# Block means by a second accumulated product instead of a broadcast transfer, in the first four units of a sparse attention followed by two gated layers

## The chip, the cores and the metric

One core of one Trainium2 chip. The metric is device time in microseconds (us) of one execution; the time of a kernel is the median over its runs. The profile is of one further execution, whose own time and span stand in the table below. The engines are PE (TensorE), DVE (VectorE), ACT (ScalarE), POOL (GpSimd) and SP, which in this kernel only issues transfers.

## The reference

Attention over 2 batches, 8 heads, 768 positions of 64 numbers, then two dense gated layers on 1536 tokens. Each query sees its neighbours closer than 16 positions and one summary for every block of 32 positions: the largest key of the block and the mean of its values.

```python
k_sum = k.reshape(B, H, nb, block, D).max(axis=3)
v_sum = v.reshape(B, H, nb, block, D).mean(axis=3)
...
scores_all = np.concatenate([scores_l_m, scores_s], axis=-1)
...
v_all = np.concatenate([v, v_sum], axis=2)
return np.matmul(a, v_all).astype(np.float32)
...
x = _moe_ref(x=x, **moe_kwargs)
return _moe2_ref(x=x, **moe2_kwargs)
```

## The kernel before

The attention is cut into 24 units: 2 batches, 3 groups of four query blocks (64 queries each), 4 pairs of heads. Units 0 to 3 are the first group, 4 to 7 the second, and so on; batch 1 begins with unit 12. One unit goes through these steps, each a function:

- `w_copy` (POOL, tile `kx`): the window of 96 keys of each query block, and ahead of it 32 columns for the block maxima (`ks`, made by DVE in `prep_k`).
- `b_pe` (PE, L556 and L558, tile `ps_s`): a product that adds the mask, then four score products of the unit's queries `q` with `kx`. `b_max` (DVE, `nm`), `b_exp` (ACT, `e`), `n_inv` (DVE) and `n_mul` (POOL) make the weights.
- `c_pe` (PE, L591, `ps_p`) transposes them, `c_copy` (ACT for the first ten units, `pt`) copies them out.
- `d_pe` (PE, L606, `ps_x`): eight products per unit of `pt` with `vwin`. `d_hi` (ACT, `xH`) and `d_lo` (DVE, `xL`) split the result into two parts for the dense layers.

`vwin` has eight slots of 128 rows, four for one group and four for the next: rows 32 to 127 hold the window's values, loaded by `load_v` (L495), and rows 0 to 31 the block means, which `put_v` (L500) copies into all four slots of a group by a transfer from the tile `vsum` (named `vs` in the trace). The means come from `sum_load` (transfers, `vt`), `sum_v` (DVE sums, `vm`), and `sum_lay` (four PE products `ps_v`, then ACT at L530). For batch 0, `put_v(0, 0)` and `put_v(0, 1)` are issued by ACT, the others by SP.

Weights of the dense layers come by `fetch` (L165, 1 MB pieces named `raw`, one in the tile `xH`) and are decoded into two parts each by DVE and ACT (`decode`, L102 to L112). Their products are at L349; those of the first layer on the first 512 tokens can begin when units 0 to 7 are done.

The order on PE, DVE, ACT and POOL is set by a scheduler when the program is built, so an edit at one place can move instructions elsewhere; each engine then runs its list in order. SP's list stands in the order in which the code is written. The query loads of units 0 to 3 are issued by ACT, all other loads by SP. The transfers share eight completion semaphores in turn: a transfer that takes one waits until its last user has landed. Queries have five buffers, so the load of unit u waits for the scores of unit u - 5. The first `load_v` of batch 0's third group overwrites the slots of the first group, and waits in SP's list for the last `ps_x` of unit 3; behind it stand that group's `put_v`, the queries of unit 13, and the weight piece `raw_1_1` of `moe_w_out`.

Of the kernel before, what the change touches and what calls it, by code (L numbers as in the profile page):

```python
# [8 lines left out]
F32 = mybir.dt.float32  # L9
# [3 lines left out]
AF = mybir.ActivationFunctionType  # L13
# [3 lines left out]
P = 128  # L17
# [11 lines left out]
def attention_moe_moe2_kernel(ctx: ExitStack, tc: tile.TileContext, ins: dict, out: bass.AP):  # L29
    nc = tc.nc  # L30
# [4 lines left out]
    B, HP, _, S = vt.shape  # L35
    H, D = 2 * HP, 64
    BLK = 32
# [4 lines left out]
    W0 = 32  # L42
    M0 = W0 + HALO
    G = 4
# [7 lines left out]
    scale = 1.0 / float(D) ** 0.5  # L52
# [98 lines left out]
    for layer, g, i in wanted:  # L151
        w = mats[layer][i]
        last = i == len(mats[layer]) - 1
        x = w.bitcast(U32)
        pieces.append((f"{layer}_{g}_{i}", rows_of(x, g) if last else cols_of(x, g, 2)))

    def fetch():

        if pieces:
            name, src = pieces.pop(0)  # L160
            n, m = src.shape[1], src.shape[2]

            home, tag = (xp, "xH") if name == "1_0_1" else (wraw, "raw")
            raw = home.tile([P, n * m], U32, tag=tag, name=f"{tag}{name}")
            nc.sync.dma_start(out=raw.rearrange("p (a n) -> p a n", a=n), in_=src)  # L165
            raws.append((raw, (P, n, m // 2)))
# [279 lines left out]
    def pull(n):  # L446
        for _ in range(n):
            if next(coming, True):
                break
# [5 lines left out]
    with tc.manual_schedule(engines={mybir.EngineType.SP}), ExitStack() as es:  # L455
# [6 lines left out]
        vp = es.enter_context(tc.tile_pool(name="a_v", bufs=1))  # L462
        ps_a = es.enter_context(tc.tile_pool(name="ps_a", bufs=1, space=PSUM))

        vwin = one.tile([P, 2 * G, H * D], F32, name="vwin")
# [4 lines left out]
        qbd, vsum, kraw, kmax, kx = {}, {}, {}, {}, {}  # L470
        SH = S + 2 * HALO

        def load_k(b, hp):

            t = kp.tile([P, SH], F32, tag="k", name=f"k{b}_{hp}")
            nc.sync.dma_start(out=t, in_=k[b, hp])
            kraw[b, hp] = t

        def load_q(u, eng):

            b, g, hp = units[u]
            t = qp.tile([P, G, P], F32, tag="q", name=f"q{u}")
            eng.dma_start(out=t.rearrange("p i c -> p (i c)"), in_=q[b, g, hp])
            qbd[u] = t

        def vw(b, i):
            return vwin[:, (b * NG + i // G) % 2 * G + i % G, :]

        def load_v(b, g):
            c = (b * NG + g) % 2 * G  # L490
            first_row = v[b, g * G * QB:g * G * QB + P - W0, :]
            src = bass.AP(
                first_row.tensor, first_row.offset, [first_row.ap[0], [QB * H * D, G], [1, H * D]]
            )
            nc.sync.dma_start(out=vwin[W0:P, c:c + G, :], in_=src)  # L495

        def put_v(b, g, eng=nc.sync):
            c = (b * NG + g) % 2 * G
            src = vsum[b].unsqueeze(1).to_broadcast([W0, G, H * D])
            eng.dma_start(out=vwin[0:W0, c:c + G, :], in_=src)  # L500

        vtl, vpart = {}, {}

        def sum_load(b, hp):
            if (b, hp) == (0, 2):
                early = xp.tile([P, 2, KC * TB // 2], F32, tag="xL", name="vt_early")
                vtl["early"] = [early[:, i, 0:S] for i in range(2)]
            if b == 0 and hp > 1:
                t = vtl["early"][hp - 2]
            else:  # L510
                t = vp.tile([P, S], F32, tag="vt", bufs=2, name=f"vt{b}_{hp}")
            nc.sync.dma_start(out=t, in_=vt[b, hp])
            vtl[b, hp] = t

        def sum_v(b, hp):
            if hp == 0:
                vpart[b] = vp.tile([P, HP, W0], F32, tag="vm", name=f"vm{b}")
                nc.vector.memset(vpart[b], 0.0)
            nc.vector.tensor_reduce(
                out=vpart[b][:, hp, 0:NB], in_=vtl.pop((b, hp)).rearrange("p (n t) -> p n t", t=BLK),  # L520
                axis=AX.X, op=ALU.add,
            )

        def sum_lay(b):
            r = vpart.pop(b)
            vsum[b] = vp.tile([W0, H * D], F32, tag="vs", name=f"vs{b}")
            ps = ps_a.tile([W0, H * D], F32, tag="x", name="ps_v", bufs=2)
            for hp in range(HP):
                nc.tensor.matmul(ps[:, hp * P:(hp + 1) * P], lhsT=r[:, hp], rhs=ident, start=True, stop=True)
            nc.scalar.activation(vsum[b], ps, AF.Copy, scale=1.0 / BLK)  # L530

        def prep_k(b, hp):
            ks = kp.tile([P, W0], F32, tag="ks", name=f"ks{b}_{hp}")
            nc.vector.memset(ks, 0.0)
            own = kraw[b, hp][:, HALO:HALO + S].rearrange("p (n t) -> p n t", t=BLK)
            nc.vector.tensor_reduce(out=ks[:, 0:NB], in_=own, axis=AX.X, op=ALU.max)
            kmax[b, hp] = ks
# [61 lines left out]
        def d_pe(u):  # L599
            b, g, hp = units[u]  # L600
            t = live.pop(("pt", u))
            ps = ps_a.tile([P, G, QB], F32, tag="x", name="ps_x", bufs=2)
            for j in range(G):
                for e in range(2):
                    h = 2 * hp + e
                    nc.tensor.matmul(  # L606
                        ps[64 * e:64 * e + 64, j, :],
                        lhsT=vw(b, g * G + j)[:, h * D:(h + 1) * D],
                        rhs=t[:, j, 64 * e:64 * e + 64],
                        start=True, stop=True,  # L610
                    )
            live["x", u] = ps.rearrange("p j c -> p (j c)")

        def x_slice(x, u):
# [11 lines left out]
        def d_lo(u):  # L626
# [6 lines left out]
        ORDER = [  # L633
            (w_copy, -1), (b_pe, 0), (b_max, 0), (n_inv, LN), (n_mul, LN),
            (c_pe, LC), (c_copy, LC), (d_pe, LD), (d_hi, LD), (b_exp, 0), (d_lo, LD),
        ]


        warm = one.tile([P, TB], BF16, name="warm")
        nc.vector.memset(warm, 0.0)  # L640
        for _ in range(4):
            ps = ps_h.tile([P, TB], F32, tag="h", name="ps_w")
            nc.tensor.matmul(ps, lhsT=warm[:, 0:P], rhs=warm, start=True, stop=True)
# [52 lines left out]
        for t in range(-1, NU + LD):  # L696
            now[0] = t

            u = t + 2
            if u < NU and units[u][1] == 0:  # L700
                prep_k(units[u][0], units[u][2])
            for part, lag in ORDER:
                if 0 <= t - lag < NU:
                    part(t - lag)
            if 0 <= t < NU - 5:
                load_q(t + 5, nc.sync)
            if t == -1:
                sum_v(0, 0)
                sum_v(0, 1)
            if t == 0:  # L710
                sum_v(0, 2)
                sum_v(0, 3)
                sum_lay(0)
                put_v(0, 0, nc.scalar)
                load_v(0, 1)
                put_v(0, 1, nc.scalar)
                fetch()
            if t in (5, 8):
                fetch()
            if t in (7, 8, 9, 10):  # L720
                sum_load(1, t - 7)
            if t in (8, 9, 10, 11):
                sum_v(1, t - 8)
            if t == 11:
                sum_lay(1)

            if t % HP == HP - 1 and HP < t < NU - HP:
                c = t // HP + 1
                load_v(c // NG, c % NG)
                put_v(c // NG, c % NG)  # L730
            if 8 <= t < 8 + HP:
                load_k(1, t - 8)
            if t >= 1:
                pull(1 if t < 6 or t > 9 else 2)
            for _ in range(2 if t >= 8 else 1):
                next(fill, None)
# [3 lines left out]
    with tc.manual_schedule(engines={mybir.EngineType.SP}):  # L740
# [11 lines left out]
        for step in steps[EARLY:]:  # L752
            layer, g, blk = step
# [91 lines left out]
```

## Time and profile before

| | before |
|---|---|
| median of 3 runs | 639.03 us (637.85 to 639.6) |
| the profiled execution, its time | 637.64 us |
| its span | 635.8 us |
| PE busy | 611.7 us (96%) |
| DVE busy | 431.8 us (68%) |
| ACT busy | 283.2 us (45%) |
| POOL busy | 194.3 us (31%) |

PE is busy nearly all the time after the first 70 us; the profiled execution's time lies 1.8 us above its span. Times within the trace count from the span's start.

### The profile page before, as it was taken

The numbers are of one execution on the slowest core, as the hardware profiler recorded it, in microseconds if no ns is written. First come the engines' busy times: TensorE is split into PE (matmuls) and PEld (weight loads), VectorE is DVE, ScalarE is ACT, GpSimd is POOL, SyncE is SP. The second block draws the span as 40 slices with busy tenths as digits, with TensorE's granted clock in tenths as the row PEclk, the third lists the DMA queues.
The fourth block names the chain that finished last, engine by engine and source line by source line (L and its number), as shares of the span: only waits on it lengthen the run. The fifth ranks groups of instructions, "written<-read, shape, count | busy, mean of one in ns | idle before, by whom it ended". The sixth has DMA issues, their size and how long they took to land.

```text
span 635.8 us, 8219 instructions
## 1 busy us (share of the span) xinstructions
PE 611.7 (96%) x3098; PEld 499.7 (79%) x3098; DVE 431.8 (68%) x628; ACT 283.2 (45%) x560; POOL 194.3 (31%) x164
## 2 busy tenths in 40 slices
PE   7488999999999999999999999999999999999997
PEld 4376777778888888888888887888887888888886
DVE  6788665378987575566359996169499479496524
ACT  2587676736543333323144745444344244343310
POOL 6885676313313231322222121030031030130210
PEclk9899899999999999999999999999999999999999
DMA  9989653014542212100002304012122112200004
GB/s 307 330 269 333 227 134 67 2 66 149 183 132 67 66 67 66 67 1 1 0 1 66 109 25 132 1 66 66 67 67 74 59 67 66 68 0 1 1 34 165
DMA packets 25304, 58.33 MB, mean 92 GB/s; under 512 B 1585, under 2 KB 1841, under 8 KB 25265
## 3 DMA queue, kind: packets, MB, share of 16 engines
q1 hardware_dynamic: 24400, 56.24, 27.3%
q10 hardware_dynamic: 864, 1.57, 0.7%
q8 instruction: 24, 0.39, 0.3%
q14 instruction: 16, 0.12, 0.1%
HBM read 53.08 MB, written 3.15 MB: 88 GB/s over the span
## 4 chain that ended last, share of the span: by engine, by line
PE 82%; DVE 7%; ACT 3%; DMA 3%; POOL 2%; issue 2%; SPq 0%; ACTq 0%; DVEq 0%; POOLq 0%
PE ps_o L349 34%; PE ps_h L349 19%; PE ps_v L124 8%; PE ps_y L124 7%; PE ps_x L124 5%; PE ps_h L124 4%; PE ps_s L558 3%; DMA raw<-in_moe_w_out 2%; POOL kx L547 1%; PE ps_x L606 1%; DVE wf L205 1%; DVE ws L214 1%; DMA vt<-in_vt 1%; PE ps_p L591 1%; DVE sg L364 1%
## 5 line engine op out<-in xcount | busy, mean ns | idle before, releaser
L366 POOL TENSOR_TENSOR gl<-sg,gh 128x512 fp32r<-128x512 f32 x84 | 119.5, 1424 | 404.3 <-ACT gh L365 381.0
L429 DVE TENSOR_TENSOR acc<-ps_o,acc 128x512 f32<-128x512 f32 x143 | 97.2, 686 | 57.2 <-PE ps_o L349 57.1
L365 ACT CAST gh<-sg 128x512 fp32r<-128x512 f32 x84 | 51.9, 620 | 91.7 <-DVE sg L364 81.2
L349 PE MATMUL ps_h<-xL,w_0H 128*128 128x512 f32 x192 | 75.1, 391 | 1.5 <-DVE xL L627 1.5
L349 PE MATMUL ps_h<-xH,w_0L 128*128 128x512 f32 x192 | 75.1, 394 | 0.3 <-DVE acc L429 0.3
L349 PE MATMUL ps_o<-gl,w_1H 128*128 128x512 f32 x192 | 75.3, 392 | 0.1
L349 PE MATMUL ps_o<-gh,w_1L 128*128 128x512 f32 x192 | 74.8, 398 | 0.2 <-DVE sg L364 0.2
L349 PE MATMUL ps_o<-gh,w_1H 128*128 128x512 f32 x192 | 74.8, 390 | 0.0
L349 PE MATMUL ps_h<-xH,w_0H 128*128 128x512 f32 x192 | 74.8, 389 | 0.0
L364 DVE TENSOR_TENSOR sg<-ps_h,sg 128x512 f32<-128x512 f32 x48 | 33.0, 687 | 47.0 <-ACT sg L373 46.9
L349 PE MATMUL ps_o<-w_2H,gl 128*128 128x512 f32 (+1 forms) x146 | 56.2, 389 | 1.0 <-ACT acc L425 0.6
L349 PE MATMUL ps_o<-w_2L,gh 128*128 128x512 f32 (+1 forms) x146 | 56.4, 386 | 0.0
L349 PE MATMUL ps_o<-w_2H,gh 128*128 128x512 f32 (+1 forms) x146 | 56.4, 386 | 0.0
L373 ACT ACTIVATE sg<-ps_h 128x512 f32<-128x512 f32 x48 | 28.4, 595 | 60.7 <-PE ps_h L349 60.6
L107 DVE SCALAR_TENSOR_TENSOR da<-da,db 128x1024 uint32<-128x1024 uint32 x34 | 43.8, 1287 | 13.8 <-ACT da L103 13.5
L103 ACT ACTIVATE da<-da 128x1024 f32<-128x1024 f32 x34 | 36.1, 1060 | 32.6 <-DVE da L102 29.8
L349 PEld LDWEIGHTS ps_h<-xL,w_0H 128*128 128x128 f32 x192 | 36.1, 188 | 9.1 <-DVE xL L627 1.9
L349 PEld LDWEIGHTS ps_h<-xH,w_0L 128*128 128x128 f32 x192 | 36.0, 188 | 8.0 <-DVE acc L429 0.8
L349 PEld LDWEIGHTS ps_o<-gh,w_1L 128*128 128x128 f32 x192 | 36.1, 189 | 7.8 <-DVE sg L364 0.5
L349 PEld LDWEIGHTS ps_o<-gl,w_1H 128*128 128x128 f32 x192 | 36.1, 188 | 7.6 <-POOL gl L366 0.4
L349 PEld LDWEIGHTS ps_o<-gh,w_1H 128*128 128x128 f32 x192 | 36.1, 188 | 7.3
L349 PEld LDWEIGHTS ps_h<-xH,w_0H 128*128 128x128 f32 x192 | 36.0, 188 | 7.3
(157 smaller groups left out, 1236.5 us busy)
## 6 DMA issues: line engine op xcount, KB each, us to landing
raw<-in_moe_w_out SPq DMA_DIRECT2D x13, 1024.0 KB, 4.8
raw<-in_moe_w_in SPq DMA_DIRECT2D x8, 1024.0 KB, 7.3
raw<-in_moe_w_gate SPq DMA_DIRECT2D x6, 1024.0 KB, 5.1
raw<-in_moe_w_val SPq DMA_DIRECT2D x6, 1024.0 KB, 5.2
q<-in_q SPq DMA_DIRECT2D x20, 256.0 KB, 7.8
vwin<-in_v SPq DMA_DIRECT2D x6, 768.0 KB, 7.8
k<-in_k SPq DMA_DIRECT2D x8, 400.0 KB, 7.3
out<-acc SPq DMA_DIRECT2D x11, 256.0 KB, 2.0
```

The source lines that it names most:

```text
L103: nc.scalar.activation(af, af, AF.Prelu, scale=REBIAS, alpha=-2.0 ** 32)
L107: nc.vector.scalar_tensor_tensor(out=a, in0=a, scalar=3, in1=b, op0=ALU.logical_shift_left, op1=ALU.bitwise_or)
L124: nc.tensor.matmul(ps, lhsT=a[x][:, kk, :], rhs=b[y][:, kk, :], start=start and i == 0, stop=i == n - 1, skip_group_check=True,)
L205: nc.vector.tensor_tensor(out=w.rearrange(flat), in0=hi.rearrange(flat), in1=lo.rearrange(flat), op=ALU.add)
L214: nc.vector.tensor_tensor(out=s[:, n], in0=a, in1=b, op=op)
L349: nc.tensor.matmul(ps, lhsT=a, rhs=b, start=i == 0, stop=i == n - 1)
L364: nc.vector.tensor_tensor(out=sg, in0=val, in1=sg, op=ALU.mult)
L365: nc.scalar.copy(gh, sg)
L366: nc.gpsimd.tensor_tensor(out=gl, in0=sg, in1=gh, op=ALU.subtract)
L373: nc.scalar.activation(sg, ps, AF.Sigmoid, scale=1.702 if layer == 1 else 1.0)
L429: nc.vector.tensor_tensor(out=a[:, m, :], in0=ps, in1=a[:, m, :], op=ALU.add)
L558: nc.tensor.matmul(ps[:, j, :], lhsT=t[:, j, :], rhs=kt[:, j, :], start=False, stop=j == G - 1)
```

## The change

The tile `vsum` gets 128 rows and a buffer for each batch. ACT fills, at the start, rows 0 to 31 of the first four slots of `vwin` and the whole of batch 0's `vsum` with zeros, from the zero tile `warm`; later `sum_lay` writes the means into rows 0 to 31 of `vsum`, and the rest stays zero. Units 0 to 3 then take two products into the same accumulator: `pt` with `vwin`, whose mean rows are zero, and `pt` with `vsum`, whose window rows are zero. The transfer `put_v(0, 0)` is no longer issued. All other units work as before.

```diff
         def put_v(b, g, eng=nc.sync):
             c = (b * NG + g) % 2 * G
-            src = vsum[b].unsqueeze(1).to_broadcast([W0, G, H * D])
+            src = vsum[b][0:W0].unsqueeze(1).to_broadcast([W0, G, H * D])
             eng.dma_start(out=vwin[0:W0, c:c + G, :], in_=src)
...
+        for b in range(B):
+            vsum[b] = vp.tile([P, H * D], F32, tag="vs", bufs=B, name=f"vs{b}")
...
         def sum_lay(b):
             r = vpart.pop(b)
-            vsum[b] = vp.tile([W0, H * D], F32, tag="vs", name=f"vs{b}")
...
-            nc.scalar.activation(vsum[b], ps, AF.Copy, scale=1.0 / BLK)
+            nc.scalar.activation(vsum[b][0:W0], ps, AF.Copy, scale=1.0 / BLK)
...
                     h = 2 * hp + e
-                    nc.tensor.matmul(
-                        ps[64 * e:64 * e + 64, j, :],
-                        lhsT=vw(b, g * G + j)[:, h * D:(h + 1) * D],
-                        rhs=t[:, j, 64 * e:64 * e + 64],
-                        start=True, stop=True,
-                    )
+                    parts = [(vw(b, g * G + j), t)]
+                    if (b, g) == (0, 0):
+                        parts.append((vsum[b], t))
+                    for n, (x, y) in enumerate(parts):
+                        nc.tensor.matmul(
+                            ps[64 * e:64 * e + 64, j, :],
+                            lhsT=x[:, h * D:(h + 1) * D],
+                            rhs=y[:, j, 64 * e:64 * e + 64],
+                            start=n == 0, stop=n == len(parts) - 1,
+                        )
...
         nc.vector.memset(warm, 0.0)
+        nc.scalar.copy(vwin[0:W0, 0:G, :], warm[0:W0].unsqueeze(1).to_broadcast([W0, G, H * D]))
+        nc.scalar.copy(vsum[0], warm)
...
                 sum_lay(0)
-                put_v(0, 0, nc.scalar)
                 load_v(0, 1)
                 put_v(0, 1, nc.scalar)
```

The scheduler moves the products of units 0 to 3. In the order of before they all stand behind the scores of units 6 and 7. These are rows of PE's list of before, from the mask product ahead of unit 6 on (`kx6`, `q6` belong to unit 6; `ps_x_302`, `_348`, `_391`, `_435` are units 0, 1, 2, 3):

```order
L556 MATMUL ps_s_464<-mask_110,pick_111 128x512
L558 MATMUL ps_s_415<-kx6_368,q6_246 128x128 x4
L556 LDWEIGHTS pick_111
L556 MATMUL ps_s_513<-mask_110,pick_111 128x512
L558 MATMUL ps_s_464<-kx7_412,q7_276 128x128 x4
L606 MATMUL ps_x_302<-pt_300,vwin_109 64x64 x8
L606 MATMUL ps_x_348<-pt_346,vwin_109 64x64 x8
L558 MATMUL ps_s_513<-kx8_461,q8_321 128x128 x4
L591 MATMUL ps_p_428<-ident_67,e_315 128x128 x4
L606 MATMUL ps_x_391<-pt_389,vwin_109 64x64 x8
L606 MATMUL ps_x_435<-pt_433,vwin_109 64x64 x8
```

Now the first product of unit 0 (`ps_x_304`, line 611 of the changed file) stands ahead of the scores of units 3 and 4, and its partner with `vs0` behind the transposes of unit 1:

```order
L611 MATMUL ps_x_304<-pt_302,vwin_109 64x64
L530 MATMUL ps_v_213<-ident_67,vm0_185 32x128
L559 MATMUL ps_s_338<-kx4_281,q4_150 128x128 x4
L559 MATMUL ps_s_284<-kx3_256,q3_142 128x128 x4
L530 MATMUL ps_v_213<-ident_67,vm0_185 32x128
L592 MATMUL ps_p_351<-ident_67,e_243 128x128 x4
L611 MATMUL ps_x_304<-pt_302,vs0_112 64x64
```

From there the pairs of units 0 and 1 follow one another, then the scores of unit 5, then the pairs of unit 2. Further on in the changed list, the last pair of unit 2 (`ps_x_409`) comes just ahead of the scores of units 6 and 7, and unit 3 (`ps_x_461`) just behind:

```order
L611 MATMUL ps_x_409<-pt_407,vs0_112 64x64
L559 MATMUL ps_s_441<-kx6_386,q6_248 128x128 x4
L559 MATMUL ps_s_498<-kx7_438,q7_278 128x128 x4
L557 LDWEIGHTS pick_111
L557 MATMUL ps_s_547<-mask_110,pick_111 128x512
L611 MATMUL ps_x_461<-pt_459,vwin_109 64x64
L611 MATMUL ps_x_461<-pt_459,vs0_112 64x64
```

So three of the four units moved ahead of unit 6's scores, and the fourth ahead of unit 8's. The second place is the head of ACT's list. Before, it issues four query loads and then loads its function table:

```order
L483 DMA q0_122<-in_q 128x512
L483 DMA q1_126<-in_q 128x512
L483 DMA q2_132<-in_q 128x512
L483 DMA q3_138<-in_q 128x512
L571 ACT_TABLE_LOAD
```

In the changed list the table load and the two zero copies stand between the second and the third query load:

```order
L483 DMA q0_126<-in_q 128x512
L483 DMA q1_130<-in_q 128x512
L646 ACT_TABLE_LOAD
L646 CAST vwin_109<-warm_114 32x2048
L647 CAST vs0_112<-warm_114 128x512
L483 DMA q2_136<-in_q 128x512
L483 DMA q3_142<-in_q 128x512
```

The table load is the same one, moved ahead. SP's list keeps its order over the stretch that the prediction speaks of.

## Rows read from the trace of the kernel before

**Rows 1.** Chain of work that ended last, 30 to 60 us: start, length, what.
```profile
34.24 1.32 PE ps_x L606 x32
...
37.11 0.59 ACT pt L596
...
40.37 10.12 DMA raw<-in_moe_w_out
...
50.51 0.69 DVE db L105
```

**Rows 2.** Stretches: busy time (and instructions) by engine, then clock, DMA share, GB/s.
```profile
20.00:30.00 10.00, 3.40 (x21) 2.03 (x20) 8.16 (x13) 7.38 (x28) 9.94 (x9) 0.89 1.05 301
30.00:36.00 6.00, 5.94 (x53) 5.53 (x54) 4.74 (x9) 2.97 (x5) 4.58 (x5) 0.61 1.04 369
36.00:38.00 2.00, 1.94 (x34) 1.63 (x35) 1.66 (x6) 1.16 (x5) 1.93 (x2) 1.00 0.80 284
38.00:40.00 2.00, 1.86 (x27) 1.55 (x23) 1.55 (x5) 2.00 (x9) 1.36 (x2) 1.00 0.25 40
40.00:42.00 2.00, 1.08 (x8) 0.65 (x7) 2.00 (x4) 2.00 (x11) 1.58 (x2) 1.00 0.74 202
42.00:50.00 8.00, 7.07 (x82) 6.17 (x83) 5.18 (x12) 7.73 (x35) 4.60 (x4) 1.00 1.05 320
50.00:60.00 10.00, 8.53 (x74) 6.38 (x72) 9.49 (x17) 5.90 (x19) 6.32 (x6) 1.00 1.05 387
...
32.00:34.00 2.00, 2.00 (x10) 1.85 (x8) 1.86 (x2) 0.31 (x1) 2.00 (x3) 0.50 1.06 389
```

**Rows 3.** Timeline of PE, 20 to 36 us: start, length, what, idle before and releaser.
```profile
22.25 1.16 PE L558 MATMUL ps_s<-kx,q 128*128 128x128 f32 x8
...
30.06 2.05 PE L558 MATMUL ps_s<-kx,q 128*128 128x128 f32 x8 [3.50 <-POOL e L585]
...
32.32 1.91 PE L558 MATMUL ps_s<-kx,q 128*128 128x128 f32 x8
34.17 1.39 PE L606 MATMUL ps_x<-pt,vwin 128*64 128x64 f32 x32
```

**Rows 4.** Timeline of POOL, 26 to 30 us.
```profile
26.43 0.53 POOL L547 TENSOR_SCALAR kx<-ks 128x128 f32<-128x128 f32 x1
26.93 3.02 POOL L585 TENSOR_TENSOR e<-e,rr 128x512 f32<-128x512 f32 x2
```

**Rows 5.** Query loads issued at 0.7, 2.2 and 15.5 us: size, us to landing.
```profile
q<-in_q ACTq DMA_DIRECT2D x1, 256.0 KB, 3.8
...
q<-in_q ACTq DMA_DIRECT2D x1, 256.0 KB, 8.0
...
q<-in_q SPq DMA_DIRECT2D x1, 256.0 KB, 14.5
```

**Rows 6.** Timeline of SP's transfers, 10 to 41 us, and its longest wait there.
```profile
10.17 0.39 SPq L165 DMA_DIRECT2D raw<-in_moe_w_in  x1
...
15.46 9.71 SPq L483 DMA_DIRECT2D q<-in_q  x5
...
38.48 0.33 SPq L495 DMA_DIRECT2D vwin<-in_v  x1
...
40.37 0.69 SPq L165 DMA_DIRECT2D raw<-in_moe_w_out  x1
...
SPq L495 <- PE ps_x L606: 3.2, 1, 3.2
```

**Rows 7.** Timeline of ACT, 0 to 23 us.
```profile
0.71 2.02 ACTq L483 DMA_DIRECT2D q<-in_q  x4
2.77 1.28 ACT L571 ACT_TABLE_LOAD   x1 [2.77 <-issue]
9.77 0.37 ACT L571 ACTIVATE e<-ps_s,nm 128x128 f32<-128x128 f32 x1 [5.71 <-DVE nm L563]
...
22.62 1.06 ACT L103 ACTIVATE da<-da 128x1024 f32<-128x1024 f32 x1 [0.67 <-DVE da L102]
```

## The prediction

> **What bounds the kernel now.** The page shows PE busy for 96% of the span, so time can only be won or lost where PE still waits, and that is the first 70 us. I therefore read first the chain of work that ended last, then the stretches around its steps, then the single engines there. The chain [rows 1] goes through the products of units 0 to 3 at 34.24 us, ACT's copy of transposed weights, the weight piece that SP issues at 40.37 and that lands 10.12 us later, and then DVE, which decodes it. The stretches [rows 2] say why a late transfer matters: the DMA share is 1.04 or more from 20 to 36 us and again from 42 to 60, so the transfers are the bound of this phase, and DVE is busy 9.49 of 10 us once the piece has landed. Between lies a hole: shares of 0.80, 0.25 and 0.74 in three stretches of 2 us leave 0.40 + 1.50 + 0.52 = 2.42 us of transfer time unused. Its cause is in SP's list [rows 6]: the window load issued at 38.48 waited 3.2 us for the last product of unit 3, and everything behind it waited too, the weight piece of 40.37 among it.
>
> Why were those products late? PE [rows 3] is idle for 6.6 of the 10 us from 20 to 30 (it is busy for 3.40 [rows 2]) and starts the scores of unit 6 at 30.06. The trace names POOL's `e` as releaser, but the scores do not read it, and their `kx` was done at 26.43 + 0.53 = 26.96 at the latest [rows 4]. What ended the wait is the query load of unit 6: issued at 15.46, landed 14.5 us later, at 29.96 [rows 5, 6]. Units 0 and 1 stand in PE's list behind units 6 and 7, so they waited for a load that they don't need.
>
> **The change, part by part.**
>
> *One transfer less.* `put_v(0, 0)` moves 256 KB, 0.262 MB. At the 301 GB/s of 20 to 30 us [rows 2] it takes 0.87 us of a full queue, and it is gone ahead of unit 6's query load in time: that load lands at about 29.1 instead of 29.96. Bounds: nothing, if its packets only filled gaps, and 0.87; I take 0.87, since the share there is 1.05. The Trainium skill (DMA: Bandwidth & Descriptors, Specifications) gives a fabric ceiling of 435 GB/s; by it the transfer would be an estimated 0.60 us and the sum below 2.8 instead of 3.1, but the trace's 301 to 389 GB/s in full stretches say that this ceiling is not reached here.
>
> *The products move.* In the changed list units 0 to 2 run in PE's idle time before 30 us and unit 3 right behind unit 7's scores. One unit of eight products is 16 records, half of the 32 that took 1.39 us [rows 3], 0.70 us; with a second product 1.39. Units 0 to 2 take 3 x 1.39 = 4.2 us, and 6.6 us are idle. Without that cover, the four units' second products would cost 4 x 0.70 = 2.8 us. They do push unit 5's scores back, from 22.25 [rows 3] by about the two units' 2.8 us less the time PE waited anyway; unit 6's query load hides that.
>
> *SP's wait ends earlier.* From 29.1 on PE does two scores and unit 3: 29.1 + 2.05 + 1.91 + 1.39 = 34.5 at the durations of rows 3, or 29.1 + 2 x 1.16 + 1.39 = 32.8 if the scores run as at 22.25. The window load that stood at 38.48 [rows 6] issues 4.0 to 5.7 us earlier, and with it the list behind it, up to the weight piece. It can win no more than the hole, 2.42 us, because the transfers around it are full. Since the share first falls between 36 and 38 and the load now comes before 35, nearly all of the hole is filled; a little stays, for the load that follows must wait for unit 8's scores. I take 2.2, with bounds 0 (something else keeps SP waiting) and 2.42. From 50 us on DVE has no idle time to give the gain back in, and its work comes forward with the piece.
>
> *The zero copies.* ACT is idle from the end of its table load, 2.77 + 1.28 = 4.05, to 9.77 [rows 7], so the time itself is free. A copy of 512 columns takes 0.59 [rows 1], an ACT instruction of 1024 columns 1.06 [rows 7]; 0.47 more for each 512 makes 2.0 us for 2048, and 2.6 for both. But queries 2 and 3 are now issued behind them: the first two issues end at 0.71 + 2 x 0.5 = 1.7, the table load at 3.0, the copies at 5.6. Query 2 goes out near 5.6 and query 3 near 6.1 instead of near 1.7 and 2.2. At 3.8 to 8.0 us to landing [rows 5] query 3 lands between 9.9 and 14.1, where it landed at 10.2, and the weight piece at 10.17 [rows 6], which reuses its semaphore, went out just then. I take zero: the two loads now travel alone in ACT's queue, and SP's own earlier transfers keep the engines full while SP waits. The upper bound is 14.1 - 10.2 = 3.9 us for all that stands behind.
>
> *The second buffer of `vsum`* only takes away a possible wait; no price.
>
> The sum is 0.87 + 2.2 = 3.1 us less. Against the profiled execution's own 637.64 that makes 634.5; the median of the runs shown, 639.03, lies 1.4 above it, and the forecast for it is **635.9 us**. A check from PE's side: the idle time from 20 to 30 takes in 4.2 us of products, of which 2.8 are new work in all, and the rest of the gain must come from waits after 36, where PE is busy only 1.08 of 2 us from 40 to 42 [rows 2]. That is enough room.
>
> **The rivals.**
>
> *The gain is given back (same).* DVE is nearly full from 50 to 60 us; if its work, and not the weight piece, sets the pace from 42 on, only the removed transfer remains: 639.03 - 0.87 = 638.2. For it speaks the 9.49 of 10; against it that DVE is busy for only 5.18 of the 8 us from 42 to 50, and that the chain enters DVE through the landing. Chance 0.22.
>
> *PE gains more (faster).* The granted clock is 0.50 from 32 to 34, half of full speed, that is 1.2 instead of 2.4 GHz, after PE had been idle most of the 10 us before [rows 2]. Scores took 2.05 and 1.91 instead of 1.16 [rows 3]. If the moved products keep the clock up, that is 1.6 us, and PE no longer does three first products of 0.70 after 30 but one more second product: 1.4 less. With the 0.87 this makes 3.9, or 635.1, if the transfers then follow; the hole's 2.42 added to the 0.87 and half of this would reach 633.5. The Trainium skill (TensorE: Matmul & The Clock Gate, What's actually happening) says the throttled state is the default and activity releases it; by that rule the fuller stretch would keep full speed, and the trace agrees as far as the 0.50 follows the idle time. Chance 0.15.
>
> *The query loads come late (slower).* Place: ACT's list at 1.7 us. If query 3 lands so late that the engines run empty while SP waits for its semaphore, all transfers behind, unit 6's queries among them, move back by up to 3.9 us: 639.03 - 0.87 + 3.9 = 642.1, and less as far as the hole is still filled. It decides from the moment the landing passes the landings of what SP had issued before. Against it: SP's transfers of that time take longer than that, as 14.5 us for a load issued at 15.46 shows [rows 5]. Chance 0.15.
>
> **How the numbers follow.** The forecast's own mechanism gets 0.48, with 635 to 637. About 0.3%, 1.9 us, is what a measurement of this kernel can tell from no change (its runs span 637.85 to 639.6), so same means 637.1 to 640.9. Faster takes 0.48 and 0.15, less a little for a forecast that falls short: 0.61. Same: 0.23. Slower: 0.16. The range reaches from the faster rival's 633 to 640.5, and leaves out most of the slow rival and some of the fast end.
>
> **What would show it.** In the changed profile: products of unit 0 before 24 us; scores of unit 6 at about 29 and near 1.2 us long if the clock held; the third window load issued before 36; no stretch with a DMA share of 0.25 near 38; the weight piece landed by 48 instead of 50.5. Wrong would be: unit 6 later than 30, query 3 landing after 13, a new hole elsewhere, or DVE without a gap and yet no earlier at 60.

## The result, and the profile after

The changed kernel took 629.80 us (median of 4 runs, 629.61 to 629.99), against 638.44 us of the kernel before on the same chip (4 runs, 637.31 to 639.6): a ratio of 0.9865, 95% interval 0.9844 to 0.9885, or 8.6 us less. The forecast was 635.9 us, with a range from 633 to 640.5. The direction was right; the gain was nearly three times the forecast's, and the time lies below the range.

The stretches of the kernel after, for [rows 2] (same columns):

```profile
20.00:30.00 10.00, 8.47 (x128) 6.97 (x127) 6.67 (x15) 7.88 (x28) 7.67 (x9) 0.94 1.05 322
30.00:40.00 10.00, 8.98 (x112) 7.10 (x110) 9.92 (x20) 8.26 (x33) 9.38 (x8) 1.00 1.05 325
36.00:38.00 2.00, 1.51 (x22) 1.21 (x23) 2.00 (x6) 2.00 (x10) 2.00 (x3) 1.00 0.89 270
38.00:40.00 2.00, 2.00 (x23) 1.50 (x24) 1.92 (x6) 2.00 (x8) 2.00 (x2) 1.00 1.06 232
40.00:42.00 2.00, 1.98 (x26) 1.75 (x22) 2.00 (x5) 1.14 (x8) 2.00 (x3) 1.00 1.08 228
50.00:60.00 10.00, 8.44 (x78) 6.52 (x77) 10.00 (x18) 9.94 (x28) 7.78 (x7) 1.00 0.89 283
```

PE is busy for 8.47 us of 20 to 30 instead of 3.40, and the granted clock is 1.00 from 30 us on. The hole in the transfers is gone: shares of 0.89, 1.06 and 1.08 where there were 0.80, 0.25 and 0.74. Over the first 140 us:

```profile
0.00:140.00 140.00, 129.13 (x1026) 99.89 (x1027) 99.67 (x197) 91.72 (x282) 89.76 (x91) 0.99 0.64 203
```

The same stretch of the kernel before:

```profile
0.00:140.00 140.00, 120.09 (x929) 93.44 (x929) 93.26 (x190) 87.84 (x276) 85.06 (x88) 0.96 0.62 196
```

PE idles 10.9 us there instead of 19.9. That is 9.0 us less; over the whole span it is busy for 613.1 instead of 611.7 us, 1.4 more, and 9.0 - 1.4 = 7.6 is, but for rounding, the 7.7 us by which the spans differ (628.1 against 635.8).

SP's transfers after, for [rows 6]:

```profile
33.62 0.33 SPq L495 DMA_DIRECT2D vwin<-in_v  x1
...
36.07 0.70 SPq L165 DMA_DIRECT2D raw<-in_moe_w_out  x1
...
63.01 0.62 SPq L500 DMA_DIRECT2D vwin<-vs  x1
```

Before, the last of these stood here:

```profile
65.26 0.61 SPq L500 DMA_DIRECT2D vwin<-vs  x1
```

So the window load came 4.9 us earlier and the weight piece 4.3, and of that only 2.25 us are left at 63 us. That is near the forecast's 2.2 us, but it is a shift of SP's list; the kernel gained 8.6. PE's timeline after shows what else moved: the first of the second products, which is unit 0's, unit 4's product, the first dense product of the first layer (`ps_h`), and the first of the second layer (`ps_o`).

```profile
22.75 0.27 PE L611 MATMUL ps_x<-pt,vs 128*64 128x64 f32 x1
...
30.23 2.05 PE L559 MATMUL ps_s<-kx,q 128*128 128x128 f32 x16
...
36.35 0.69 PE L611 MATMUL ps_x<-pt,vwin 128*64 128x64 f32 x16 [0.38 <-DVE rs L579]
...
38.97 0.73 PE L349 MATMUL ps_h<-xH,w_0L 128*128 128x512 f32 x2
...
57.34 0.50 PE L349 MATMUL ps_o<-gh,w_1L 128*128 128x512 f32 x1 [1.50 <-ACT gh L365]
```

The same in the kernel before, whose products of units 0 and 1 started at 34.17 [rows 3]:

```profile
42.93 0.69 PE L606 MATMUL ps_x<-pt,vwin 128*64 128x64 f32 x16 [1.14 <-DVE xL L627]
...
46.89 0.71 PE L349 MATMUL ps_h<-xH,w_0L 128*128 128x512 f32 x2
...
66.45 1.20 PE L349 MATMUL ps_o<-gh,w_1L 128*128 128x512 f32 x2
```

The first layer begins 7.9 us earlier and the second 9.1. That is about the size of the gain, but these starts do not carry it alone: e7 below has nearly the same start of the first layer and no gain. (The first layer's products go piece by piece along the units' order: the first need only units 0 and 4, not all of 0 to 7.) Before, unit 4's product waited for `xL` of units 2 and 3, because `ps_x` has two buffers; and in DVE's list that `xL` stood behind work that has nothing to do with it:

```profile
40.16 0.92 DVE L519 TENSOR_REDUCE vm<-vt 128x24 f32<-128x768 f32 x1
41.00 1.54 DVE L107 SCALAR_TENSOR_TENSOR da<-da,db 128x1024 uint32<-128x1024 uint32 x1
42.46 0.74 DVE L627 TENSOR_TENSOR xL<-ps_x,xH 128x256 fp32r<-128x256 f32 x2
```

### The profile page after: what moved, and what is told of

The parts are those of the page before. It is cut to its first block, busy times and chain, and to the rows that moved or that the text cites. A ratio compares the mean times of both kernels' runs of the same rounds, so it can differ in the third digit from the quotient of the medians.

```text
span 628.1 us, 8342 instructions
## 1 busy us (share of the span) xinstructions
PE 613.1 (98%) x3162; PEld 499.9 (80%) x3162; DVE 430.8 (69%) x628; ACT 282.5 (45%) x560; POOL 194.8 (31%) x164
## 4 chain that ended last, share of the span: by engine, by line
PE 86%; DVE 9%; ACT 2%; issue 1%; DMA 1%; SPq 0%; DVEq 0%; ACTq 0%
PE ps_o L349 35%; PE ps_h L349 20%; PE ps_v L124 8%; PE ps_y L124 7%; PE ps_x L124 5%; PE ps_h L124 4%; PE ps_s L559 3%; PE ps_x L611 2%; PE ps_p L592 1%; DVE wf L205 1%; DVE ws L214 1%; DMA vt<-in_vt 1%; ACT e L572 1%; DVE nm L564 1%; DVE sg L364 1%
```

## The experiments

All ratios are to the kernel before on the same chip, with 95% intervals; the changed kernel's is 0.9865. The theories that the expectations name: A, the gain is the earlier timetable of the transfers; B, it is the products that run in PE's idle time; C, B with the lists of DVE and ACT named as what the late products held; D, A and B add up; E, products and loads are two inputs of one chain, and the later one sets the pace.

**The second products and the zeros by themselves.** *e4_one_product* is the changed kernel with one product only (`parts.append` left out), so units 0 to 3 leave out the block means.

> The changed kernel without the second products: units 0 to 3 leave the block means out. PE has 2.8 us less work in the first 35 us. If the second products lie in PE's idle time, as both theories have it, the time is that of the changed kernel within 1.5 us. If they lie on the path, it is 2.8 us faster than the changed kernel, near 627.

0.9886 (0.9856 to 0.9916): as the changed kernel. PE's idle time hides the second products. *e8_zeros_only* is the kernel before with the two zero writes:

```diff
+        spare = one.tile([P, H * D], F32, name="spare")
+        nc.scalar.copy(vwin[0:W0, 0:G, :], warm[0:W0].unsqueeze(1).to_broadcast([W0, G, H * D]))
+        nc.scalar.copy(spare, warm)
```

> The kernel before with the two zero writes on ScalarE alone, one of them into a spare tile; TensorE's order is that of the kernel before. All three theories: the same as before within 0.6 us (637.3 to 638.4 us). If the start of ScalarE's list matters (query loads 2 and 3 behind the copies), up to 3 us slower.

1.0005 (0.9992 to 1.0019): no effect, as forecast.

**Products late, or early but waiting.** *e1_late_means* brings the means into `vsum` by a 64 KB transfer, so that the second products wait for a transfer again:

```diff
+            lay = vlay if b == 0 else vsum[b][0:W0]
...
+            if b == 0:
+                nc.scalar.dma_start(out=vsum[0][0:W0], in_=vlay)
```

> The changed kernel, but the block means reach the zero-padded tile by a transfer of 64 KB on ACT's queue, so the second products of units 0 to 3 wait for a transfer again and the scheduler puts them behind unit 7's scores, as before. Both products are computed. Theory A (the gain is SP's timetable: the window load no longer waits, 2.2 to 2.4 us, and one transfer less, 0.9): only the transfer saved counts, about 0.9 us faster than before. Theory B (the gain is PE's list: products of units 0 to 3 run while PE waits for unit 6's queries, and the dense products behind come earlier): the gain is gone, between 1 us faster and 2.8 us slower than before, since the second products now lie on PE's path. A gain above 5 us would speak against both.

1.0042 (1.0021 to 1.0063). The scheduler puts the pairs behind unit 7's scores again, and the whole gain is gone. Both things are late there: those pairs start at 33.08, the window load at 39.89. *e5_products_first* is the kernel before with a rule of order only: the scores of units 6 to 8 behind the products of units 0 and 1.

```diff
+                if u in (6, 7, 8) and j == 0:
+                    tc.add_manual_dep(x.ins, last[1].name, mybir.DependencyInfo(mybir.DependencyClass.NoSync, mybir.DependencyReason.DATA), reason="order")
```

> The kernel before, with one rule more for the scheduler: the scores of units 6, 7 and 8 stand behind the products of units 0 and 1. Nothing is computed otherwise, the transfer of the means stays, and it lands near 29, just before unit 6's queries. Theory A: SP's window load comes 1 to 2 us earlier, gain 0 to 2 us. Theory B: about 1.4 us of products leave the stretch after 30 us and the list behind changes with them; gain 2 to 6 us. No gain would say that what stands behind in the list, and not the place of these products, made the difference.

1.0100 (1.0069 to 1.0130), 7 us slower than before. The products still wait for the means' transfer, and the scores now wait with them:

```profile
28.93 1.98 PE L608 MATMUL ps_x<-pt,vwin 128*64 128x64 f32 x32
```

That is 5.2 us earlier than 34.17, and the first layer began 1.7 us earlier (45.16 instead of 46.89); but the window load came 1.6 us later (40.07) and the second layer 2.2 (68.66). So earlier products of units 0 and 1 were not enough for a gain here, and an early place in a list did not bring them ahead of their data.

**The clock.** *e13_kept_warm* is the kernel before with 15 products of the zero tile in PE's idle time; their results are not read.

```diff
+            for _ in range(15 if u == 6 else 0):
+                spare = ps_h.tile([P, TB], F32, tag="h", name="ps_w")
+                y = nc.tensor.matmul(spare, lhsT=warm[:, 0:P], rhs=warm, start=True, stop=True)
```

> The kernel before with 15 products of the zero tile (128 x 512, bf16) in TensorE's idle time ahead of unit 6's scores, 25 to 30 us; their results are not read, and the order of all else is that of the kernel before. TensorE's granted clock at 30 to 35 us should be 1.00 instead of 0.50. If the clock lost after the idle time is part of the gain: 2 us faster than before, 635.5 to 636.5 us. If it is not on the path: the same as before within 0.6 us.

1.0032 (1.0015 to 1.0049). The stretch from 30 us in the kernel before, the same in e13, and e13's two first dense products:

```profile
30.00:40.00 10.00, 9.75 (x104) 8.72 (x105) 7.95 (x17) 6.13 (x16) 7.87 (x7) 0.76 0.83 286
```

```profile
30.00:40.00 10.00, 8.18 (x108) 6.88 (x106) 9.57 (x17) 7.10 (x24) 9.68 (x9) 1.00 0.81 265
```

```profile
44.27 0.71 PE L349 MATMUL ps_h<-xH,w_0L 128*128 128x512 f32 x2
...
65.97 1.22 PE L349 MATMUL ps_o<-gh,w_1L 128*128 128x512 f32 x2 [2.42 <-ACT gh L365]
```

The clock was 1.00 there instead of 0.76, the products of units 0 and 1 came at 31.67 instead of 34.17 and the first layer 2.6 us earlier, and still the kernel was 2.3 us slower. A clock kept up by itself gained nothing with products this late. Whether the clock is a part of the gain once they are early, no run shows. Why the second layer came only 0.5 us earlier is not settled; PE idled 4.4 of the 10 us from 60 on.

**The transfers' timetable, with the products late.** *e3_twelve_slots* is the kernel before with twelve window slots instead of eight (`3 * G`, and `% 3`), so that the window load waits for no product.

> The kernel before, with twelve slots in vwin instead of eight, so that the third group's window load overwrites nothing that is still read and SP does not wait for unit 3's product; PE's list is unchanged. Theory A: the window load issues near 35 instead of 38.5, and the kernel gains 2 us or more, to about 636. Theory B: the transfers come earlier but PE's list does not change, so less than 1.5 us of gain.

1.0050 (1.0032 to 1.0068). The window load:

```profile
35.42 1.55 SPq L495 DMA_DIRECT2D vwin<-in_v  x1
```

It came 3.1 us earlier than before and the weight piece, at 38.53, 1.8 us; the DMA share of 30 to 40 rose from 0.83 to 0.96, and nothing was gained. This is where theory A fell. Why the kernel was even 3.7 us slower (640.98 against 637.32) is not settled. *e12_late_twelve* has the second products and no transfer, but PE's order of before (units 0 and 1 behind unit 7's scores, 2 and 3 behind unit 8's), and twelve slots:

```diff
+                if 0 <= t - lag < NU and not (part in LATE and 3 <= t < 8):
...
+                if part is b_pe and t in (7, 8):
+                    for u in ((0, 1), (2, 3, 4))[t - 7]:
+                        for p in LATE:
+                            p(u)
...
-        vwin = one.tile([P, 2 * G, H * D], F32, name="vwin")
+        vwin = one.tile([P, 3 * G, H * D], F32, name="vwin")
```

> The run before this one (products late in TensorE's list, no transfer), and twelve window slots instead of eight, so that the window load waits for no products and comes at 33 to 35 us: timetable early, products late. Theory A: 629 to 631 us. Theory B: 636 to 640 us. Theory D: about 636 us.

0.9999 (0.9982 to 1.0016). *e14_late_and_held* adds a hold of SP's queue:

```diff
+                if t == 7:
+                    nc.sync.dma_start(out=mark, in_=live["sum", 7])
```

> The run with late products and twelve window slots, with SyncE's queue held ahead of the window load by the tiny transfer of unit 7's sums: late products and late timetable, but no transfer of means. Theory E (two inputs of one chain: the later one sets the pace, so that making one of them early is worth little while the other is late): the same as the kernel before and as the run without the hold, 637 to 640 us. Theory D (the two terms add up): 4.3 us slower than the run without the hold, about 642 us.

0.9994 (0.9980 to 1.0008). With late products unit 7's sums are late too, so the hold was far longer than planned. The window load of e12, then that of e14:

```profile
32.61 0.42 SPq L495 DMA_DIRECT2D vwin<-in_v  x1
```

```profile
44.22 0.58 SPq L495 DMA_DIRECT2D vwin<-in_v  x1
```

They lie 11.6 us apart, and the two kernels take the same time. But they are not a clean pair. Their stretches from 40 us, e12, then e14:

```profile
40.00:50.00 10.00, 10.00 (x125) 8.83 (x122) 7.00 (x15) 8.95 (x38) 5.15 (x5) 0.76 0.99 306
```

```profile
40.00:50.00 10.00, 9.72 (x127) 8.30 (x128) 7.35 (x18) 10.00 (x45) 5.39 (x5) 1.00 0.39 92
```

The granted clock was 0.76 in e12 and 1.00 in e14, and e14, with the later load, began the first layer 2.2 us earlier (47.82 against 50.01) and the second 3.7 (65.55 against 69.25). In e14 the chain of work that ended last goes through the weight piece behind the held load, as it did in the kernel before:

```profile
46.30 10.07 DMA raw<-in_moe_w_out
```

In e12 it goes through DVE and PE instead. So an early window load gains nothing while the products are late (e3, e12); that a late one then costs nothing is what the times say, but not shown with all else equal. *e10_products_late*, the same order with eight slots, was flawed: the products of units 2 and 3 stand behind the window load that overwrites their slots, so they read the later window and wait for it.

> The changed kernel, without the transfer and with the second products, but TensorE's list in the order of the kernel before: the products of units 0 and 1 behind unit 7's scores, those of units 2 and 3 behind unit 8's. The window load then waits for unit 3's products again, to 38 us or so. Theories B and D: the gain goes, 636 to 640 us. Theory A: also 637 to 638 us, since the window load is late. If it stays under 632 us, the order of the products is not what counts, but the transfer as such.

1.0065 (1.0046 to 1.0085); it tells nothing that e12 does not.

**The transfers' timetable, with the products early.** *e7_sp_held* and *e11_held_to_38* are the changed kernel with the same kind of hold, behind unit 4's `xL` and behind unit 7's sums.

```diff
+                    nc.sync.dma_start(out=mark, in_=x_slice(xL, 4)[:, 0:64].bitcast(F32))
```

> The changed kernel, with a tiny transfer of unit 4's lower half xL on SyncE's queue ahead of the window load, so that SyncE is held about as late as in the kernel before (window load at about 38 us instead of 33.6 us) while TensorE's order stays. Theory A: the 2.4 us or more that the earlier timetable gives are lost, 632 us or more, and nearly all of the 8.6 us if the timetable is the whole gain. Theories B and C: 629.8 us, at most 1 us more.

> The changed kernel with SyncE's queue held ahead of the window load by a tiny transfer of unit 7's sums (128 x 4), which are ready at about 37.7 us: window load at about 38.3 us, as in the kernel before, and TensorE's order that of the changed kernel. Theory A (the timetable of the transfers is the whole gain): 637 to 638 us. Theory B (the products in TensorE's idle time are the whole gain): 629.5 to 630.5 us. Theory D (two terms: the timetable costs 0.85 us for each us that it comes later, the late products about 6 us): 631.5 to 634 us.

1.0014 (1.0000 to 1.0028) and 0.9934 (0.9912 to 0.9955). The window loads, e7 and e11:

```profile
41.53 0.53 SPq L495 DMA_DIRECT2D vwin<-in_v  x1
```

```profile
37.23 0.53 SPq L495 DMA_DIRECT2D vwin<-in_v  x1
```

That is 7.9 and 3.6 us later than in the changed kernel, and the times are 8.2 and 4.3 us longer (638.02 and 634.13 against 629.80; these are from different chips, on which the kernel before itself ran from 637.06 to 638.44). Here the timetable counts, about one for one. In e7 the whole gain is gone although its products of units 0 and 1 start at 22.75, as in the changed kernel, and its two dense layers here:

```profile
38.98 0.73 PE L349 MATMUL ps_h<-xH,w_0L 128*128 128x512 f32 x2
...
60.62 1.20 PE L349 MATMUL ps_o<-gh,w_1L 128*128 128x512 f32 x2
```

That is 7.9 and 5.8 us earlier than in the kernel before, for the same time. So early products alone gain nothing, and theories B and C fall too. In e7 the hold was longer than meant and left the transfers idle:

```profile
36.00:38.00 2.00, 1.50 (x22) 1.19 (x23) 2.00 (x6) 2.00 (x10) 2.00 (x3) 1.00 0.07 29
38.00:40.00 2.00, 2.00 (x23) 1.50 (x24) 1.92 (x6) 2.00 (x8) 2.00 (x2) 1.00 0.00 0
```

In e11 the chain of work that ended last shows who paid, DVE, whose list waited for a value load:

```profile
40.00 10.48 DMA vt<-in_vt
50.48 0.02 issue
50.50 0.04 DVE vm L522
...
52.05 0.34 DVE xL L633
52.39 0.04 issue
52.44 1.39 PE ps_h L349 x4
```

e11 began the first layer at 37.94, a little before the changed kernel, and the second at 59.47, 2.1 us behind it.

**Other ways to bring the means early, and the bytes.** *e9_direct*: the kernel before, with one copy by ACT instead of the transfer and no second products.

```diff
+            if b == 0:
+                nc.scalar.copy(vwin[0:W0, 0:G, :], vsum[b].unsqueeze(1).to_broadcast([W0, G, H * D]))
...
-                put_v(0, 0, nc.scalar)
```

> The kernel before, with the transfer of the means into slots 0 to 7 replaced by one copy on ScalarE (32 x 2048) straight from the tile of means; no second products and no zeros. Theory A (the gain is the earlier window loads and fewer bytes on the transfers' timetable): window load at about 33.6 us instead of 38.5 us, 630 us. Theory B (the gain is that TensorE's first products run in its idle time at 20 to 30 us): the products of units 0 and 1 run right behind the copy, some 2 us later than in the changed kernel, 630 to 631 us. Theory C (each engine works its list in order, and the lists of VectorE and ScalarE were held by late products): the same, 630 to 631 us, with ScalarE busy over 8 us of 30 to 40 us. If instead the form with two products matters by itself, 636 us or more.

0.9916 (0.9890 to 0.9941), 632.25 us: most of the gain without the second products, with the products of units 0 and 1 at 25.07 instead of 22.75 and the window load at 34.17. *e2_traffic_back* puts the 256 KB transfer back into the changed kernel, to a tile that nobody reads (`nc.scalar.dma_start(out=spare, ...)`), and *e15_second_copy* takes the next group's transfer out of it:

```diff
-                put_v(0, 1, nc.scalar)
+                nc.scalar.copy(vwin[0:W0, G:2 * G, :], vsum[0][0:W0].unsqueeze(1).to_broadcast([W0, G, H * D]))
```

> The changed kernel, plus the same 256 KB transfer of the means on ScalarE's queue, into a spare tile that nobody reads: the bytes are back, the wait for them is not. Theory A in its form as traffic (the fabric has 256 KB less to move): 0.9 to 2.2 us of the gain go, 631 to 632 us. Theories B and C (what counts is that the products no longer wait for a transfer): 629.8 us within 0.6 us. At 637 us or more the bytes alone would be the cause.

> The changed kernel, with the transfer of the means for units 4 to 7 (256 KB on ScalarE's queue) replaced by one copy on ScalarE (32 x 2048, about 2 us). If the traffic counts as the run with the spare transfer says (256 KB more made it 4.2 us slower): up to 4 us faster than the changed kernel, 626 to 629 us. If ScalarE's 2 us at 23 us delay the exponentials as much: 629.5 to 632 us.

0.9948 (0.9928 to 0.9967), 634.0 us, and 0.9942 (0.9924 to 0.9960), 634.29 us. In e2 the window load moved to 36.90. In e15 the window load came at 35.19, and the copy stood in the middle of ACT's exponentials, for which PE waited:

```profile
23.47 1.89 ACT L722 COPY vwin<-vs 32x2048 f32<-32x2048 f32 x1
```

```profile
29.28 0.38 PE L557 MATMUL ps_s<-mask,pick 128*128 128x512 bf16 x1 [2.46 <-ACT e L572]
```

Both lose more than half of the gain. None of these versions beats the changed kernel.

## Why the prediction was wrong

The two inputs side by side, from the runs above (ratio to the kernel before, and when the window load was issued):

| | load at 32 to 34 us | load at 37 to 39 us | load after 41 us |
|---|---|---|---|
| products early (units 0 and 1 by 22.75 us) | 0.9865 (changed, 33.62) | 0.9934 (e11, 37.23) | 1.0014 (e7, 41.53) |
| products late (units 0 and 1 from 31.66 us on) | 0.9999 (e12, 32.61) | 1 (before, 38.48) | 0.9994 (e14, 44.22) |

Only where both are early is there a gain of that size; either one alone gives nothing. So A, B, C and D fail (D would have put e14 at 642 us; it took 637.55). Theory E, two inputs of which the later one sets the pace, fits this table best of the theories named. It is not shown to the end: by the one for one of e7, the load at 44.22 alone would put e14 near 640.7 us, and e14 took 637.55; and e5 and e13 had their products and their first layer earlier than the kernel before and were still slower.

**The step that failed is the first: "the transfers are the bound of this phase".** A DMA share of 1.04 to 1.05 was read as a bound, and the hole at 36 to 42 us as lost time on the path, so that the change "can win no more than the hole, 2.42 us". With late products, an earlier load that fills the hole gains nothing (e3, e12). With early products it comes with 8.6 us, and in e7, where the products are as early and the load is late, the 8.6 us are gone. So the term for SP's wait was wrong both ways, and the earlier products had no term at all. By which path they set the pace is argued from the traces only: over the two `ps_x` buffers and DVE's `xL` to the first dense products. No run changes that path by itself.

Point by point:

- *The products move, hidden in PE's idle time.* Right: e4 shows the second products to be free. But the move was priced only through SP's wait. That the products themselves come earlier (those of units 0 and 1 by 11.4 us, 22.75 instead of 34.17), and with them the dense layers, had no term in the sum. The reason given for their lateness was also only half of it: they stood behind unit 6's scores, but their own means, sent at 21.20, landed 7.8 us later, at 29.0, one us ahead of those scores.
- *SP's wait ends earlier*, by 4.0 to 5.7 us: measured 4.9. The hole is filled, as forecast. Once the products are early, 3.6 us of it are worth 4.3 us (e11), and alone it is worth nothing (e3, e12), so neither 2.2 nor 0 is "its" value.
- *One transfer less*, 0.87 us by unit 6's query load: nothing by that way. The load landed at 15.16 + 15.0 = 30.16 instead of 29.96. Yet the same bytes put back cost 4.2 us (e2), with the window load 3.3 us later, which the forecast did not see.
- *The zero copies*: free, as taken (e8), but not for the reason given. Queries 2 and 3 were not issued at 5.6 and 6.1 us; their issue began at 1.73 (last section). The slow rival had no ground.
- *The rival "PE gains more"* named the right engine and, in 633.5, came nearest. (Its terms do not give that number: 0.87 + 2.42 and half of 3.9 come to 633.8.) That it came nearest is luck as far as the clock goes, which kept up alone gained nothing (e13).
- *The rival "same"* asked whether DVE's work sets the pace from 42 us on. DVE did get fuller: it is busy for 9.92 of 30 to 40 us and 10.00 of 50 to 60, where it was 7.95 and 9.49, and the chain that ended last runs through it from 46.61 to 62.43. The gain was not given back by it.
- *The signs.* Unit 0's products before 24 us, the window load before 36, no hole and the weight piece landed by 48 (36.07 + 10.1 = 46.2) all came. So did one of the signs of being wrong, unit 6's scores later than 30 (30.23), and the gain came all the same.

What stays open: by which waits the early products and the early loads together gain 8.6 us, how the 4.3 us of e11 divide between the two waits of DVE there, and why e3, e5 and e13 lost time. The changed kernel's chain has little slack left in any direction: 2 to 4 us on a transfer (e2, e11) or on ACT (e9, e15) cost it 2.4 to 4.5 us, while the differences among kernels with late products, up to 7 us from 0.9994 (e14) to 1.0100 (e5), were not taken apart.

## What to carry to other kernels

A resource that is full is not yet the bound, and a hole in it is not yet lost time: before a gap is priced, follow both inputs to the step where they meet (here the units' results and what SP loads) and ask which comes later. An edit that frees an instruction from a wait needs a term for the consumers of its result, and not only for the other wait that it also ends. And of two late inputs each can look worthless when it alone is repaired (e7, e12), so both must be moved together before either is judged. This change did that with one edit: SP's window load waited for the very products that it moved.

## What the runs showed of the hardware that was not expected

ACT issued two query loads while its own earlier instructions still ran. The timeline of the changed kernel:

```profile
0.71 0.90 ACTq L483 DMA_DIRECT2D q<-in_q  x2
1.65 1.28 ACT L646 ACT_TABLE_LOAD   x1 [1.65 <-PEq L840]
1.73 1.10 ACTq L483 DMA_DIRECT2D q<-in_q  x2
2.94 1.90 ACT L646 CAST vwin<-warm 32x2048 f32<-32x2048 bf16 x1
4.74 0.61 ACT L647 CAST vs<-warm 128x512 f32<-128x512 bf16 x1
```

The loads stand behind both copies in ACT's list and began at 1.73, under the table load. The forecast had them queue behind 4 us of work. The Trainium skill (Perfetto Trace Analysis, Sequencer Loop) says that a sequencer reads the next instruction, pushes an engine instruction into a queue, and starts a control instruction itself. If the issue of a transfer counts as the latter, the trace agrees as far as these two issues go, which did not wait for the copies ahead of them.

The transfer engines' full stretches moved from 228 GB/s (the changed kernel, 40 to 42 us, DMA share 1.08) to 387 (the kernel before, 50 to 60, share 1.05), so the share alone does not say how much is being moved.
